# A fused attention and expert-lookup kernel: two of the four blocks of the input turned by transposing DMAs in the opening

## The chip, the cores and the metric

The kernel runs on one core of a Trainium2 chip. The metric is the device time of one execution in microseconds (us), lower is better. The core has five engines that work through instruction streams of their own and meet at semaphores: TensorE (PE; its weight loads are shown as PEld), VectorE (DVE), ScalarE (ACT), GpSimd (POOL) and SyncE (SP), from which nearly all DMAs are issued.

## The reference

```python
def _A_ref(x, wqkv, wo):                       # D = 448, 16 heads of 28
    qkv = (x @ wqkv).reshape(B, S, 3, H, Dh) ...
    p = softmax(einsum("bhqd,bhkd->bhqk", q, k) * Dh ** -0.5)
    return einsum("bhqk,bhkd->bhqd", p, v) ... @ wo
...
x = A_x                                        # 1 x 2048 x 448, float32
h = x + _A_ref(_layernorm(x), A_wqkv, A_wo)
h2 = h + _B_ref(_layernorm(h), ...)            # top-8 of 64 x 64 product keys per head,
                                               # gelu(x . u[e]) weighted, times v[e]
```

Only the opening is touched: layernorm of x, then keys, values and queries for the attention. Each fp32 factor of these products is carried as two fp16 parts (high and low), and a product is the sum of high*high, high*low and low*high.

## The kernel before

**Tiling.** The 2048 rows of x are four blocks of 512 rows, each of four tiles of 128 rows. `normed(b)` loads nothing; it takes a block that `load_x` has brought to `xb` (two buffers, so `load_x(b + 2)` stands at its end), makes mean and variance on VectorE (L395, L396), the reciprocal root on GpSimd (L110, L113) and the normalised tile `xn` on VectorE (L116). The products need x with features on the partitions, so each tile is turned: four TensorE transposes into PSUM (`turn`, L122, tile `tr`), the high parts by ScalarE from PSUM (L97, into `XH`), the low parts by VectorE from PSUM (`lows`, L136 and L137, into `XL` and into the free half of `XH`'s fourth slab).

**The order of the work.** `qkv()` normalises blocks 0 and 1. Then it runs over the four blocks: `keys(0, b)` (11 matmuls of 512 columns into `pq`; squares, a norm bound `kmax`, and the result split into `fh` and `fl` and stored) and, for blocks 0 and 1, `values_of(b)` (four times 11 matmuls of 448 columns, result `vst`, stored in `vd`). Blocks 2 and 3 are normalised inside that loop, ahead of `keys(0, 1)` and `keys(0, 2)`. The rest follows: `queries(0, b)`, then keys and queries of the other three groups of four heads, and the values of blocks 2 and 3 at the end. Keys of all four blocks must stand before the first query is finished, since `kmax` is taken over them. All of `qkv()` is laid out by a scheduler; it fixes an order per engine, GpSimd's alone is as written. Attention and all that comes after have an order written out by hand.

**Two helpers that stand ready.** `natural` (L127 to L130) splits a normalised tile where it lies, with its features along the free dimension: two casts for the high parts, two subtractions for the low ones, seven slabs of 128 columns in the order that `XH` and `XL` have. It is used later in the kernel (`project`), where a DMA of the transposing kind (L699) then turns those seven slabs, 128 rows x 896 columns of fp16 (229 KB), from SBUF to SBUF.

**Pools.** `wk` holds two buffers of each name (`bufs=2`) unless a tile asks for more: `xn` has two. `ps` holds two buffers of `tr` and four of `pq`.

## Time and profile before

| | us |
|---|---|
| median of 3 runs (lowest, highest) | 1591.58 (1589.65, 1596.7) |
| the profiled execution's own time | 1590.46 |
| its span, first to last instruction | 1588.7 |
| start of the first matmul of `keys(0, 1)` in that span | 37.9 |
| start of the first matmul of `keys(0, 2)` | 51.4 |
| start of the first matmul of `keys(0, 3)` | 55.2 |

The lines of the profile that carry the argument stand in the prediction. In them "L122 PE MATMUL tr<-ct,xn" is line, engine, operation, tile written <- tiles read (buffer numbers left out). Times at the start of a timeline row are us from the start of the span; "x4" groups instructions that follow each other; what stands in square brackets is the engine's idle time before the row, and what ended it. A row of a group ends with busy us and mean ns, or with the shortest, median and longest duration in ns. A DMA's row on SPq is the time that SyncE took to issue it; "to landing" counts from the start of that issue to the last completion.

### The profile page before, as it was taken

How to read it: one execution, taken by the hardware profiler on the slowest of the kernel's cores; microseconds unless marked ns; L12 is line 12 of the kernel's file. 1: busy time of each engine (PE TensorE's matmuls, PEld its weight loads, DVE VectorE, ACT ScalarE, POOL GpSimd, SP SyncE). 2: the span in 40 equal slices, each digit the busy share in tenths (PEclk: the TensorE clock that was granted, in tenths of full speed). 3: DMA queues.
4: the chain of work that ended last, by engine and by line, in shares of the span. 5: the costliest groups of instructions: out<-in, count | busy, mean ns of one | idle time of the engine just before them, and what ended most of it. 6: DMA issues, size and time to landing. Idle time of an engine off the chain costs nothing.

```text
span 1588.7 us, 33185 instructions
## 1 busy us (share of the span) xinstructions
PE 1532.8 (96%) x12540; PEld 669.4 (42%) x12540; DVE 1146.5 (72%) x3924; ACT 910.0 (57%) x1220; POOL 362.1 (23%) x488
## 2 busy tenths in 40 slices
PE   5999999999999999999998999999999999999999
PEld 3444222233333333333335654455445554555444
DVE  7763365444477867666599899789998999789623
ACT  3544888888888888888873433344423344334322
POOL 1242000534235743787662000000000000000000
PEclk9999999999999999999999999999999999999999
DMA  8424687556677756569733244453344534443444
GB/s 278 141 97 127 224 268 244 173 179 215 213 252 218 245 173 219 165 202 278 225 114 101 91 133 130 130 182 119 105 136 129 158 107 132 141 137 117 121 144 134
DMA packets 170018, 266.10 MB, mean 167 GB/s; under 512 B 25472, under 2 KB 102016, under 8 KB 169856
## 3 DMA queue, kind: packets, MB, share of 16 engines
q1 hardware_dynamic: 165632, 261.88, 52.9%
q10 hardware_dynamic: 4224, 2.10, 0.4%
q8 instruction: 98, 1.61, 0.4%
q14 instruction: 64, 0.52, 0.1%
HBM read 211.88 MB, written 49.28 MB: 164 GB/s over the span
## 4 chain that ended last, share of the span: by engine, by line
PE 74%; DVE 18%; DMA 2%; POOL 2%; issue 2%; ACT 1%; SPq 0%; DVEq 0%; POOLq 0%
PE M L93 14%; PE acc L1234 14%; PE A L592 13%; PE S L565 11%; PE A L93 9%; PE pq L93 6%; DVE p L994 4%; DVE fg L979 2%; DVE G L1015 2%; PE M L273 2%; PE A L1021 1%; DVE ring L1206 1%; DVE f L973 1%; DVE w L1209 1%; PE A L1011 1%
## 5 line engine op out<-in xcount | busy, mean ns | idle before, releaser
L569 ACT ACTIVATE P<-S,escale 128x1024 f32<-128x1024 f32 x512 | 535.7, 1118 | 82.1 <-PE S L565 75.9
L1234 PE MATMUL acc<-v,w 128*128 128x448 f16 x1536 | 308.3, 354 | 1.3 <-DVE w L1209 1.0
L592 PE MATMUL A<-P,V 128*32 128x512 f32 x2048 | 257.6, 601 | 1.3 <-DVE o L597 1.3
L565 PE MATMUL S<-qS,kS 32*128 32x512 f16 x3072 | 230.4, 378 | 2.9 <-ACT P L569 2.2
L1234 PEld LDWEIGHTS <-w 128*128 128x128 f16 x1536 | 148.4, 98 | 143.4 <-DVE w L1209 4.0
L93 PEld LDWEIGHTS <-u 128*128 128x128 f16 x1386 | 131.1, 98 | 146.4 <-issue 6.8
L93 PE MATMUL A<-Xb,u 128*128 128x512 f16 x759 | 178.6, 384 | 2.5 <-DVE G L1015 2.5
L1160 ACT ACTIVATE ring<-A,ugelu 128x512 f32<-128x512 f32 x71 | 48.7, 687 | 218.8 <-PE A L93 218.8
L994 DVE TENSOR_TENSOR p<-st,iota 128x2048 f16<-128x2048 f16 x128 | 156.7, 1225 | 14.9 <-PE M L1011 8.1
L93 PE MATMUL M<-w,Xb 128*128 128x512 f16 x704 | 163.1, 379 | 3.5 <-DVE oh L137 1.6
L1206 DVE SCALAR_TENSOR_TENSOR ring<-ring,wscale,G 128x512 f32<-128x512 f32 x128 | 92.1, 746 | 77.7 <-ACT ring L1160 77.6
L565 PEld LDWEIGHTS <-kS 32*128 32x128 f16 x3072 | 63.6, 92 | 198.3 <-issue 162.7
L93 PE MATMUL M<-Xb,u 128*128 128x512 f16 x627 | 146.4, 379 | 0.0
L93 PEld LDWEIGHTS <-Xb 128*128 128x128 f16 x704 | 64.0, 98 | 92.8 <-issue 20.5
L1208 ACT ACTIVATE w<-ring 128x512 f16<-128x512 f32 x128 | 75.8, 622 | 41.1 <-DVE ring L1206 28.9
L592 PEld LDWEIGHTS A<-P,V 128*32 128x32 f32 x2048 | 48.2, 108 | 120.5 <-issue 110.9
L816 DVE MAX8 ti<-fresh 128x8 f32<-128x64 f32 x384 | 57.3, 212 | 53.8 <-ACT fresh L797 53.6
L1051 POOL TENSOR_SCALAR raw<-raw,scale 128x512 f32<-128x512 f32 (+1 forms) x64 | 47.4, 741 | 188.7 <-PE M L158 145.8
L1209 DVE SCALAR_TENSOR_TENSOR w<-w,ring 128x512 f16<-128x512 f16 x128 | 84.9, 686 | 7.2 <-ACT w L1208 6.9
L1160 ACT ACTIVATE ring<-M,ugelu 128x512 f32<-128x512 f32 x57 | 39.2, 688 | 87.8 <-PE M L93 86.1
L979 DVE TENSOR_TENSOR fg<-f,st 128x2048 f16<-128x2048 f16 x64 | 78.8, 1231 | 0.1
L818 DVE FIND_INDEX8 ti<-ti,fresh 128x8 uint32<-128x64 f32 x384 | 76.9, 220 | 0.0
(197 smaller groups left out, 1897.3 us busy)
## 6 DMA issues: line engine op xcount, KB each, us to landing
v<-vs SPq DMA_DIRECT2D x128, 336.0 KB, 2.9
u<-us SPq DMA_DIRECT2D x126, 256.0 KB, 2.6
w<-wp SPq DMA_DIRECT2D x56, 512.0 KB, 4.9
kS<-ks SPq DMA_DIRECT2D x64, 256.0 KB, 4.9
V<-vd SPq DMA_DIRECT2D x64, 256.0 KB, 3.6
wr<-in_wq_dram SPq DMA_DIRECT2D x32, 448.0 KB, 4.2
vs<-hl SPq DMA_DIRECT2D x32, 336.0 KB, 5.2
seen<-in_uT_dram SPq DMA_DIRECT2D x32, 256.0 KB, 5.0
```

The costliest lines, as they stand in the source:

```text
L93: nc.tensor.matmul(ps, l, r, start=i == 0, stop=i == len(pairs) - 1)
L565: nc.tensor.matmul(S[j // 2][:, j % 2], kS[r, a, 128 * (k % 4):128 * (k % 4) + 128], qS[r, c], start=m == 0, stop=m == 2)
L569: nc.scalar.activation(Pt[:, 2 * i:2 * i + 2], S[i], AF.Exp, scale=escale[:, n % 4:n % 4 + 1])
L592: nc.tensor.matmul(O[n][32 * j:32 * j + 32], V[:, k % 4, j], Pt[:, j], start=k == 0, stop=k == NT - 1)
L818: nc.vector.max_index(i, t, src)
L979: nc.vector.tensor_tensor(fg.rearrange("p t k f u -> p t k (f u)"), f1.rearrange("p t f u -> p t (f u)").unsqueeze(2).to_broadcast([128, T ...
L994: newest[0] = nc.vector.tensor_tensor(p1, pairs(0, s, TG, 128), ids(TG, 128), op=OP.is_equal).ins
L1160: gelu[0] = nc.scalar.activation(act, p, AF.Gelu_apprx_tanh, scale=ugelu).ins
L1206: nc.vector.scalar_tensor_tensor(av, av, wscale, of_expert(b, f), op0=OP.mult, op1=OP.mult)
L1208: nc.scalar.activation(w[:, 0], a, AF.Copy, scale=1.0 / LS)
L1209: newest[0] = nc.vector.scalar_tensor_tensor(w[:, 1], w[:, 0], -LS, a, op0=OP.mult, op1=OP.add).ins
L1234: nc.tensor.matmul(acc[j][:, :D], l, r, start=f == 0 and k == 0, stop=f == 31 and k == 2)
```

## The change

Blocks 2 and 3 are no longer turned on TensorE. VectorE splits their tiles with `natural` into `hl`, a new tile of pool `wk` with two buffers, and a transposing DMA issued from SyncE turns each into `XT[b]`. `XH` and `XL` of a block become parts of one tile `XT`, so that one DMA can write both. Blocks 0 and 1 are turned as before. In the loop `normed(b + 2)` now stands between `keys(0, b)` and `values_of(b)` for blocks 0 and 1, and the keys of blocks 2 and 3 follow behind the values of block 1.

```diff
-        XH = [wp.tile([128, 4, 512], F16, name=f"XH{b}") for b in range(NB)]
-        XL = [wp.tile([128, 3, 512], F16, name=f"XL{b}") for b in range(NB)]
+        XT = [wp.tile([128, 7, 512], F16, name=f"XT{b}") for b in range(NB)]
+        XH = [t[:, :4] for t in XT]
+        XL = [t[:, 4:] for t in XT]
...
                 xn = wk.tile([128, D], F32, name="xn")
                 norm(xt[:, j], xn, mv[:, j, 0:1], rstd[:, j:j + 1], nc.vector)
+                if b > 1:
+                    hl = wk.tile([128, 7 * 128], F16, name="hl")
+                    natural(hl, xn)
+                    nc.sync.dma_start_transpose(XT[b][:, :, c], hl)
+                    continue
                 pt = ps.tile([128, 4, 128], F32, name="tr")
                 turn(pt, xn)
...
             normed(1)
-            for b in range(NB):
-                if b in (1, 2):
-                    normed(b + 1)
+            for b in range(2):
                 keys(0, b)
-                if b < 2:
-                    values_of(b)
+                normed(b + 2)
+                values_of(b)
+            for b in (2, 3):
+                keys(0, b)
```

What the scheduler makes of it is seen in the order of the instructions. Lines behind the edit have moved by one to six (L380 is L381, L395 and L396 are L396 and L397, L437 is L443). On VectorE before, in the middle of block 2, a tile is normalised and its low parts are taken from PSUM, waiting for ScalarE:

```order
L137 TENSOR_TENSOR XH_216<-tr,XH_216 64x128
L116 TENSOR_SCALAR xn<-xb,mv,rstd 128x448 [waits DVE_49]
L396 BN_AGGR mv<-st 128x2 [waits DVE_49]
L395 BN_STATS st<-xb 128x6 [waits DMAHW6_49]
L136 TENSOR_TENSOR XL_220<-tr,XH_216 128x3x128 [waits Activation_49]
```

On VectorE after, from the normalising of block 2's third tile on (the splits of the first two tiles stand just ahead of these rows):

```order
L116 TENSOR_SCALAR xn<-xb,mv,rstd 128x448
L116 TENSOR_SCALAR xn<-xb,mv,rstd 128x448 [waits DVE_49]
L397 BN_AGGR mv<-st 128x2 x2
L396 BN_STATS st<-xb 128x6 [waits DMAHW5_49]
L396 BN_STATS st<-xb 128x6 [waits DMAHW6_49]
L381 CAST fh<-f 128x512 [waits Activation_49]
L443 TENSOR_REDUCE kmax<-tr 128x1 [waits PE_49]
L127 CAST hl<-xn 128x384 [waits DMAHW7_49,DVE_49]
L128 CAST hl<-xn 128x64
L127 CAST hl<-xn 128x384 [waits DMAHW0_49,DVE_49]
L129 TENSOR_TENSOR hl<-xn,hl 128x384 [waits DVE_49]
L130 TENSOR_TENSOR hl<-xn,hl 128x64 [waits DVE_49]
```

The tiles are split in pairs, and each cast of 384 columns from the third tile on waits for a DMA semaphore: that of the transposing DMA that still reads this buffer of `hl`.

On SyncE before, behind the values of block 0:

```order
L419 DMA vd<-vst_225 128x4x128 [waits DMAHW6_49,Activation_49]
L260 DMA wr<-in_wq_dram 128x896 x2
L234 DMA V<-vd 128x512 [waits DMAHW4_49,DMAHW6_49,DMAHW2_49,DMAHW1_49]
L384 DMA ks_61<-fh 128x512 [waits DVE_49]
L385 DMA ks_61<-fl 128x512 [waits DMAHW3_49,Pool_49]
L419 DMA vd<-vst_222 128x4x128 [waits Activation_49]
```

And after, at the same place:

```order
L425 DMA vd<-vst_221 128x4x128 [waits DMAHW6_49,Activation_49]
L409 DMA_TRANSPOSE XT_216<-hl 128x7x128 [waits DVE_49] x2
L260 DMA wr<-in_wq_dram 128x896 [waits DMAHW1_49]
L385 DMA ks_61<-fh 128x512 [waits DMAHW2_49,DVE_49]
L386 DMA ks_61<-fl 128x512 [waits DMAHW3_49,Pool_49]
L425 DMA vd<-vst_218 128x4x128 [waits DMAHW4_49,Activation_49]
L409 DMA_TRANSPOSE XT_216<-hl 128x7x128 [waits DMAHW5_49,DVE_49]
L409 DMA_TRANSPOSE XT_216<-hl 128x7x128 [waits DMAHW6_49,DVE_49]
```

The second pair of block 2 stands behind the stores of `keys(0, 1)` and a store of `vst`. The four of block 3 (`XT_217`) follow further on, the last two with the store of `fh` of `keys(0, 2)` between them.

On TensorE before, in `keys(0, 2)`, the last transposes of block 3 stand between matmuls:

```order
L93 MATMUL pq<-XH_216,wqkl 128x512
L122 MATMUL tr<-ct,xn 128x128 [waits DVE_49,Activation_49]
L122 MATMUL tr<-ct,xn 128x128 x3
L93 LDWEIGHTS wqkh
L93 MATMUL pq<-XL_220,wqkh 128x512
```

After, at the end of `keys(0, 2)` and the start of `keys(0, 3)`:

```order
L93 LDWEIGHTS wqkh
L93 MATMUL pq<-XT_216,wqkh 128x512
L442 MATMUL tr<-sq,blk 128x512 [waits DVE_49,Activation_49]
L93 LDWEIGHTS wqkh [waits DMAHW4_49,DMAHW7_49,DMAHW3_49,DMAHW1_49]
L93 MATMUL pq<-XT_217,wqkh 128x512 [waits PE_49]
```

The transposes (L122) are gone, and the first weight load of `keys(0, 3)` waits for four DMA semaphores, those of the four transposing DMAs of block 3; that of `keys(0, 2)` waits for the four of block 2 in the same way. The order of all five engines is the same from the queries of group 0 on.

## The prediction

> **What bounds the kernel now.** I read the page first, then busy time by stretch of the opening, then the timeline of that stretch, the chain that ended last, and the groups of the tiles that the change touches. The page says that TensorE is the busy engine of the whole:

> ```profile
> span 1588.7 us, 33185 instructions
> PE 1532.8 (96%) x12540; PEld 669.4 (42%) x12540; DVE 1146.5 (72%) x3924; ACT 910.0 (57%) x1220; POOL 362.1 (23%) x488
> ```

> That is an average over all stages; the change lies between 36 and 62 us. Busy us per engine, with the count, in three stretches: from the normalising of block 2 to the end of the keys of group 0, the short passage to the queries, and the rest of keys and queries:

> ```profile
> 36.50:58.00 21.50, 20.72 (x112) 11.22 (x113) 16.58 (x41) 9.24 (x16) 2.63 (x4) 1.00 0.57 174
> 58.00:66.20 8.20, 6.51 (x31) 2.73 (x28) 4.83 (x14) 5.57 (x8) 2.06 (x2) 1.00 0.42 130
> 66.20:129.70 63.50, 63.50 (x279) 27.61 (x279) 44.07 (x96) 30.75 (x50) 27.76 (x24) 1.00 0.32 106
> ```

> The first number behind the length is TensorE: 20.72 of 21.50 us, then 6.51 of 8.20, then all of 63.50. VectorE (third number) has 4.9 us to spare in the first stretch, the DMA engines are 0.57 busy. The chain of waits says the same of the later part:

> ```profile
> 43.08 7.58 PE pq L93 x40
> ...
> 66.69 2.39 PE pq L93 x11
> ...
> 127.33 2.39 PE pq L93 x11
> ```

> From 66 us on it runs through one group of 11 matmuls after the other, with no step on another engine that a late start could be made up in. So whatever the keys of block 3 lose or win is lost or won at the end of the kernel too: the time at which `keys(0, 3)` ends decides. In the timeline:

> ```profile
> 35.09 0.73 PE L93 MATMUL pq<-wvh,XL 128*128 128x448 f16 x3
> 36.37 0.94 DVE L116 TENSOR_SCALAR xn<-xb,mv,rstd 128x448 f32<-128x448 f32 x2 [0.91 <-POOL rstd L113]
> 37.03 1.06 PE L122 MATMUL tr<-ct,xn 128*128 128x128 f32 x8 [1.20 <-DVE xn L116]
> ...
> 51.38 1.03 PE L93 MATMUL pq<-XH,wqkh 128*128 128x512 f16 x4
> ...
> 55.22 1.02 PE L93 MATMUL pq<-XH,wqkh 128*128 128x512 f16 x4
> ...
> 57.41 0.81 PE L93 MATMUL pq<-XL,wqkh 128*128 128x512 f16 x3
> ```

> The values of block 0 end at 35.82, TensorE waits 1.20 us for the normalised tile of block 2, `keys(0, 2)` starts at 51.38, `keys(0, 3)` at 55.22, and its last matmul ends at 58.22.

> **What is removed.** The transposes of blocks 2 and 3 and what hangs on them, in this stretch:

> ```profile
> L122 PE MATMUL tr<-ct,xn x32: 272/273/302, 37.0 to 54.3; 128*128 128x128 f32 x32
> L97 ACT ACTIVATE XH<-tr x8: 590/598/599, 37.7 to 54.6; 128x512 f16<-128x512 f32 x8
> L136 DVE TENSOR_TENSOR XL<-tr,XH x8: 551/558/559, 38.3 to 55.2; 128x384 f16<-128x384 f32 x8
> L137 DVE TENSOR_TENSOR XH<-tr,XH x8: 292/293/294, 38.9 to 55.8; 64x128 f16<-64x128 f32 x8
> L436 PE MATMUL tr<-sq,blk x2: 506/545/584, 42.6 to 55.9; 128*128 128x512 f32 x2
> ```

> TensorE loses 32 transposes. What that is worth I take from its new sequence. From 35.82 it can go straight to `keys(0, 1)` (11 matmuls, 2.39), one `blk` product (0.5) and the values of block 1 (44 matmuls at 7.58 / 40 = 0.19, 8.34): it is at `keys(0, 2)` by 47.05 instead of 51.38. If nothing made it wait, both keys would end at 47.05 + 2.39 + 0.5 + 2.39 = 52.33, that is 5.9 us before 58.22. This is all that the edit can win. ScalarE loses 8 x 0.60 us; that wins nothing, since it is busy for 9.24 of 21.50 us there.

> **What is added.** Per tile, four VectorE instructions in place of L136 and L137, and one transposing DMA. The same operations stand later in this kernel; the first four rows are the split, the fifth SyncE's time to issue the turn, the sixth from that issue's start to landing:

> ```profile
> L127 DVE CAST hl<-xn x12: 359/656/1200, 345.2 to 720.0; 128x384 f16<-128x384 f32 x12
> L128 DVE CAST hl<-xn x12: 176/408/2126, 345.8 to 720.5; 128x64 f16<-128x64 f32 x12
> L129 DVE TENSOR_TENSOR hl<-xn,hl x12: 545/552/951, 346.3 to 721.0; 128x384 f16<-128x384 f32 x12
> L130 DVE TENSOR_TENSOR hl<-xn,hl x12: 210/599/1189, 346.8 to 721.5; 128x64 f16<-128x64 f32 x12
> L699 SPq DMA_TRANSPOSE Xb<-hl x12: 1226/1237/1362, 350.8 to 725.4; - x12
> ...
> DMA to landing us min/median/max: 3.1/3.4/5.1
> ```

> I take the shortest durations (0.36, 0.18, 0.55, 0.21), because GpSimd is busy 2.63 of 21.5 us here and the long ones fall in a stage where it works beside VectorE (an inference). A tile costs 1.30 us instead of 0.85, over eight tiles 3.6 us more on VectorE, which the 4.9 spare us would cover. VectorE's load is not the trouble; its order is. There are two buffers of `hl`, so a pair of tiles can be split only after the pair before has landed, and four such rounds stand one behind the other. Between them VectorE does what the order puts there; the durations, and GpSimd's for the root (L113, L110) and for `fl`:

> ```profile
> L150 DVE TENSOR_REDUCE tops<-wqkr 128x1 f32<-128x512 f32 x4 | 2.6, 677 | 0.0
> L382 POOL TENSOR_TENSOR fl<-f,fh 128x512 f16<-128x512 f32 x2 | 2.3, 1162 | 18.9 <-DVE fh L380 18.9
> L437 DVE TENSOR_REDUCE kmax<-tr 128x1 f32<-128x512 f32 x2 | 1.4, 692 | 0.5 <-PE tr L436 0.4
> L395 DVE BATCH_NORM_STATS2 st<-xb 128x6 f32<-128x448 f32 x2 | 1.2, 594 | 0.0
> L113 POOL TENSOR_TENSOR rstd<-rstd,lnpow 128x4 f32<-128x4 f32 x1 | 1.0, 1012 | 0.1
> L380 DVE CAST fh<-f 128x512 f16<-128x512 f32 x2 | 0.8, 422 | 0.0
> L396 DVE BATCH_NORM_AGGREGATE mv<-st 128x2 f32<-128x6 f32 x4 | 0.6, 170 | 0.0
> L110 POOL TENSOR_SCALAR rstd<-mv 128x4 f32<-128x4 f32 x1 | 0.2, 195 | 0.1
> ```

> **The four rounds, with the median landing of 3.4.**
> - First pair. Two tiles normalised by 36.37 + 0.94 = 37.31. The order is cast, small cast, cast of the second tile, then the two subtractions: the first `hl` is ready 1.66 later at 38.97, the second after 0.94 more at 39.91. SyncE issues one turn in 1.24, so at 38.97 and 40.21; they land at 42.4 and 43.6.
> - Second pair. 39.91 + 0.94 (normalising) + 0.34 (two L396) + 1.19 (two L395) + 0.42 (`fh`) + 0.69 (`kmax`) = 43.49. Both buffers are just free. Ready at 45.15 and 46.09. Three stores stand ahead on SyncE (`fh`, `fl`, `vst`); they should be through before 45, since `fh` is made at 42.8 and GpSimd's `fl` 1.16 later. Issued at 45.15 and 46.39, landed at 48.55 and 49.8. TensorE has waited for `keys(0, 2)` since 47.05: **2.7 us lost**.
> - Third pair. 46.09 + 0.34, then GpSimd's 1.21 for block 3's root, 0.94 to normalise, two maxima of weights (2 x 0.68): 49.94, both landed. Ready at 51.60 and 52.54, issued at 51.60 and 52.84, landed at 55.0 and 56.2.
> - Fourth pair. 52.54 + 0.94 + 0.68 + three small ones (0.5, an estimate from L396's 0.17) = 54.66, and the buffer at 55.0. Ready at 56.30; the second tile's split has the cast of `fh` between its parts: 56.30 + 1.72 = 58.02. The last turn lands at 61.4. `keys(0, 2)` and its `blk` product are over by 52.7: **8.7 us lost**.

> `keys(0, 3)` ends at 61.42 + 2.39 = 63.8 instead of 58.2, **5.6 us later**; the same from TensorE's side is 2.7 + 8.7 lost less 5.9 won, 5.5. Successive VectorE instructions overlap a little (two normalisations take 0.94, one 0.51, so 0.08 each), and some of that lies on the path, for which I take off 0.6: **+5.0 us**. Behind it nothing changes: the squares, `kmax` and the scale of the next weights hang on the end of `keys(0, 3)` as before.

> Other edits. SyncE issues eight more DMAs, 9.9 us, beside the sum; the loads of `wr` behind them are for a later stage. The low share of GpSimd stays. One tile `XT` for two costs nothing: the readers wait for the same writers.

> **Bounds of the unknown, the landing.** The nearest rows are the twelve turns, 3.1 to 5.1, one at a time; here two follow each other, beside loads of `wr`. With 3.1 the same rounds give +5.0 (+4.4 with the overlap). With 5.1 every round waits for its landing: the turns land at 45.3, 52.8, 60.2 and 67.1 (the last of each pair), and the end comes 11.3 us later. Even at the shortest plain DMA of this size the rounds stand:

> ```profile
> h<-xt SPq DMA_DIRECT2D x12, 224.0 KB, 2.0
> xb<-in_x_dram SPq DMA_DIRECT2D x16, 224.0 KB, 4.2
> ```

> With a landing of 2.0, VectorE alone sets the rounds, and the sum is +3.9. I take 3.4, the median of the same instruction with the same size. [...]

> **The rivals.**
> - *The turns land late.* The place is the two waits for `hl` and the four DMAs that a key group waits for; behind the loads of `wr` each landing takes 4.3 or more instead of 3.4. From there the loss passes 8.0 us (at 4.2 it is 7.7), which is 0.5%, about what a measurement of this kernel can tell from no change. At 5.1 throughout, 1591.6 + 11.3 = 1602.9. For it: `wr` and the stores share the queue, and the DMA engines are 0.57 busy. Against it: half of the twelve turns landed within 3.4, and one late turn is not enough, it must be one in nearly every round.
> - *All is hidden.* TensorE never waits, and the 5.9 us are won: 1585.7. For it: VectorE has room, and a longer lead (the values of block 1, 8.3 us, stand between). Against it: the rounds above would have to be 9 us too long, and even a landing of 2.0 leaves +3.9.
> - *The loss is taken up behind.* Between 58 and 66.2 TensorE is idle for 8.20 - 6.51 = 1.7 us. If what it waits for there did not hang on `keys(0, 3)`, that much of the delay would vanish: 1594.9. Against it: the passage begins with the square of `keys(0, 3)` itself.
> - *The change does not do what it says.* Excluded: the order shows the DMAs in SyncE's stream and no L122 after block 1.

> **How the numbers follow.** The sum is made against the profiled execution (1590.46, span 1588.7); the median of the runs is 1.1 higher, and the difference is added to it: 1591.58 + 5.0 = **1596.6**. Chances: the forecast (landing of 3.1 to 4.3, 4 to 8 us later) 0.62; late 0.18; taken up behind 0.10; hidden 0.08; a gain beyond what the rows allow 0.02. The forecast, the third and the hidden case are all within 0.5%: same 0.80, slower 0.18, faster 0.02. The range leaves out the hidden case and the worst of the late one: 1591 to 1602.

> **What would show it.** Right: TensorE's first weight load of `keys(0, 2)` waits 2 to 3 us and that of `keys(0, 3)` 7 to 9 us for the DMA `XT<-hl`; VectorE's casts to `hl` begin close to 43.5, 50, 55; the turns land in 3.1 to 4.3 us; the values of block 1 end near 47; from the first query on all rows stand about 5 us later, to the end. Wrong: turns at 5 us or more, or a second turn that waits for the first; splits at their long durations (2.2 us a tile instead of 1.3, which would add about 0.9 in each of the last two rounds); or waits of TensorE that are gone by 66 us.

## The result, and the profile after

| | before | after |
|---|---|---|
| median of 8 runs each, us (lowest, highest) | 1593.06 (1589.65, 1596.7) | 1599.72 (1597.16, 1602.56) |
| the profiled execution's own time, us | 1590.46 | 1598.57 |
| its span, us | 1588.7 | 1596.8 |

The changed kernel takes 1.0036 times as long (95% interval 1.0025 to 1.0047): 0.36%, which is measured but lies within the 0.5% that was called no change. Of the kernel before there are now eight runs, and their median is 1.5 us above the one that the prediction started from.

The head of the page after:

```profile
span 1596.8 us, 33142 instructions
PE 1531.1 (96%) x12508; PEld 666.0 (42%) x12508; DVE 1149.7 (72%) x3940; ACT 906.1 (57%) x1212; POOL 362.0 (23%) x488
```

Every engine has about the same work as before, TensorE is busy for 1.7 us less, and the span is 8.1 us longer. So no engine got more to do; time was lost between pieces of it. Busy time by stretch after (behind the length: PE, PEld, DVE, ACT, POOL; then the granted TensorE clock, the DMA engines' share and GB/s):

```profile
36.50:58.00 21.50, 14.83 (x65) 6.47 (x63) 18.60 (x57) 4.89 (x8) 3.77 (x4) 0.83 0.99 231
58.00:62.50 4.50, 1.59 (x4) 0.57 (x5) 0.13 (x1) 0.00 (x0) 0.00 (x0) 0.50 0.83 189
62.50:72.00 9.50, 9.06 (x37) 3.70 (x35) 4.32 (x13) 4.58 (x7) 1.16 (x1) 0.91 0.17 55
72.00:135.00 63.00, 61.77 (x271) 26.86 (x272) 42.77 (x92) 31.13 (x51) 26.61 (x23) 1.00 0.33 108
```

TensorE is busy for 14.83 of the first 21.50 us (20.72 before). In the second stretch no compute engine has work to speak of until the last turn has landed; TensorE's 1.59 us stand at its end. And there is something that stood in none of the three rows of before: a clock of 0.83 and 0.50. From 72 us on the kernel runs as it did, only later. TensorE's timeline after shows where:

```profile
46.17 0.73 PE L93 MATMUL pq<-wvh,XT 128*128 128x448 f16 x3
49.25 1.02 PE L93 MATMUL pq<-XT,wqkh 128*128 128x512 f16 x4 [2.35 <-DMA XT<-hl]
...
53.58 0.80 PE L442 MATMUL tr<-sq,blk 128*128 128x512 f32 x1 [0.69 <-ACT sq L437]
60.91 1.89 PE L93 MATMUL pq<-XT,wqkh 128*128 128x512 f16 x4 [6.54 <-DMA XT<-hl]
62.59 1.82 PE L93 MATMUL pq<-XT,wqkl 128*128 128x512 f16 x4
64.25 1.67 PE L93 MATMUL pq<-XT,wqkh 128*128 128x512 f16 x7
...
73.04 0.49 PE L454 MATMUL tr<-sq,blk 128*128 128x512 f32 x1 [1.48 <-ACT sq L452]
```

The values of block 1 end at 46.90. Then `keys(0, 2)` waits 2.35 us and `keys(0, 3)` 6.54, both for the turning DMAs. Four matmuls take 1.02 us at 49.25 and 1.89 at 60.91. The chain of waits after (start, length, what) names the rounds that caused the two waits:

```profile
42.08 0.84 DVE hl L127
...
45.38 3.62 DMA XT<-hl
49.10 0.36 DVE hl L127
...
50.09 4.06 DMA XT<-hl
54.17 0.36 DVE hl L127
...
57.55 3.31 DMA XT<-hl
60.91 5.01 PE pq L93 x15
```

A landing releases a cast into `hl`, its split releases the next turn, and the next landing again a cast: this chain holds the stretch from 45.4 to 60.9, and at its end stands `keys(0, 3)`. The same instruction (ScalarE's first square of a query) starts at 61.0 before and 68.0 after, 7.1 us later; the first softmax row of the attention at 156.2 and 163.4, 7.2 later. That row, before and after:

```profile
156.21 2.12 ACT L569 ACTIVATE P<-S,escale 128x1024 f32<-128x1024 f32 x2 [0.91 <-PE S L565]
163.37 6.38 ACT L575 ACTIVATE P<-S,escale 128x1024 f32<-128x1024 f32 x6 [0.91 <-PE S L571]
```

### The profile page after: what moved, and what is told of

Same layout as the page of the kernel before. It is cut to its first block, busy times and chain, and to the rows that moved or that the text cites. A ratio compares the mean times of both kernels' runs of the same rounds, so it can differ in the third digit from the quotient of the medians.

```text
span 1596.8 us, 33142 instructions
## 1 busy us (share of the span) xinstructions
PE 1531.1 (96%) x12508; PEld 666.0 (42%) x12508; DVE 1149.7 (72%) x3940; ACT 906.1 (57%) x1212; POOL 362.0 (23%) x488
## 4 chain that ended last, share of the span: by engine, by line
PE 64%; DVE 22%; POOL 6%; DMA 4%; issue 2%; ACT 1%; SPq 0%; DVEq 0%; POOLq 0%; ACTq 0%
PE acc L1240 13%; PE M L93 12%; PE A L598 10%; PE S L571 9%; PE A L93 8%; PE pq L93 5%; DVE p L1000 4%; DVE G L1021 2%; DVE fg L985 2%; PE M L273 2%; DVE ring L1212 2%; POOL sel L879 2%; DVE pos L824 1%; DVE w L1215 1%; POOL sel L883 1%
## 5 line engine op out<-in xcount | busy, mean ns | idle before, releaser
L93 PEld LDWEIGHTS <-u 128*128 128x128 f16 x1386 | 130.8, 98 | 145.7 <-issue 5.3
L93 PE MATMUL A<-Xb,u 128*128 128x512 f16 x759 | 175.7, 380 | 2.4 <-DVE G L1021 2.4
L93 PE MATMUL M<-w,Xb 128*128 128x512 f16 x704 | 163.1, 379 | 6.2 <-DMA w<-wp 4.2
L93 PE MATMUL M<-Xb,u 128*128 128x512 f16 x627 | 147.9, 382 | 0.0
L93 PEld LDWEIGHTS <-Xb 128*128 128x128 f16 x704 | 64.1, 98 | 95.5 <-issue 23.3
```

The lines of the kernel that those rows point to most:

```text
L93: nc.tensor.matmul(ps, l, r, start=i == 0, stop=i == len(pairs) - 1)
```

## The experiments

Delays are those of the same instruction against the profile of before. "Turns" is when the last turning DMA landed, the waits are TensorE's at `keys(0, 2)` and at `keys(0, 3)`, and "half clock" is the time at 0.5 between 36 and 80 us. Ratios are to the kernel before, on the same chip in each group of four.

| kernel | turns | waits | half clock | first softmax row | median us | ratio (95%) |
|---|---|---|---|---|---|---|
| the changed kernel | 60.9 | 2.35, 6.54 | 13.7 | +7.2 | 1599.72 | 1.0036 (1.0025, 1.0047) |
| e1: eight buffers of `hl` | 57.4 | 0.52, 6.21 | 10.2 | +4.5 | 1595.68 | 1.0019 (1.0010, 1.0028) |
| e2: work in the waits | 60.0 | none, 0.82 | 0 | +4.7 | 1597.49 | 1.0029 (1.0017, 1.0041) |
| e3: the new order alone | – | none there | 0 | +1.5 | 1594.22 | 1.0004 (0.9989, 1.0018) |
| e4: block 2 alone turned by DMA | 49.2 | none there | 3.4 | +0.7 | 1592.84 | 0.9996 (0.9986, 1.0005) |
| e5: one buffer of `hl` | 74.2 | 9.98, 10.38 | 27.3 | +20.2 | 1614.18 | 1.0116 (1.0097, 1.0135) |
| e6: values of block 2 in the hole | 61.9 | 2.42, 1.12 | 0 | -1.7 | 1591.46 | 0.9984 (0.9973, 0.9995) |
| e7: e6 with eight buffers | 60.1 | 0.39, 1.31 | 0 | -3.4 | 1587.72 | 0.9969 (0.9956, 0.9983) |
| e8: the kernel before, so filled | – | none there | 0 | +0.5 | 1593.14 | 1.0000 (0.9988, 1.0013) |

**e1: eight buffers of `hl`.** The suspected cause, taken away: no cast waits for a landing any more.

```diff
-                    hl = wk.tile([128, 7 * 128], F16, name="hl")
+                    hl = wk.tile([128, 7 * 128], F16, name="hl", bufs=8)
```

> The changed kernel with eight buffers of hl instead of two; nothing else is edited. Theory 1 (rounds): the late keys of block 3 come from four rounds of split, turn and landing that two buffers force one behind the other. With eight, the scheduler puts both pairs of a block's splits side by side: the turns of block 2 should land by 47, so TensorE does not wait for keys(0, 2), and the last turn of block 3 should land near 56.4 instead of 60.9. keys(0, 3) then ends near 60.5 (still at half clock) instead of 65.0: 4.5 us faster than the changed kernel, about 2 us slower than before. Rival (SyncE): the loss is the 9.9 us that SyncE takes to issue eight turns, in which case more buffers win nothing and the time stays about 6 us above before.

The wait at `keys(0, 2)` fell from 2.35 to 0.52 and the last turn landed 3.5 us earlier, so the two buffers did hold the rounds. They did it in two ways that this run does not part: by casts that waited for a landing, and by the order that the scheduler made for two buffers. With eight it splits the second pair of block 2 ahead of `fh`, `kmax` and the last statistics of block 3, and SyncE issues it at 42.1 instead of 44.0. The gain is smaller than expected: the attention starts 2.6 us earlier than in the changed kernel, where 4.5 had been expected of the whole time; the last landing was hoped for at 56.4 and came at 57.4. `keys(0, 3)` ran at half clock, as expected. Rows of e1, of VectorE's, SyncE's and TensorE's timeline and of the busy time:

```profile
46.43 0.94 DVE L116 TENSOR_SCALAR xn<-xb,mv,rstd 128x448 f32<-128x448 f32 x2 [0.84 <-POOL rstd L113]
51.79 1.16 SPq L425 DMA_DIRECT2D vd<-vst  x2
53.05 2.67 SPq L409 DMA_TRANSPOSE XT<-hl  x2
57.51 1.87 PE L93 MATMUL pq<-XT,wqkh 128*128 128x512 f16 x4 [6.21 <-DMA XT<-hl]
52.50:62.70 10.20, 5.19 (x13) 1.91 (x14) 2.00 (x6) 0.24 (x1) 1.15 (x1) 0.50 0.93 227
```

With the buffers free, block 3 waits for GpSimd's reciprocal root until 46.43, and its last pair of turns stands on SyncE behind two stores of `vst`. So the buffers are the first cause, and a wait of 6.21 us is left. The late start of block 3 looks like the next one; no run moved it, so that is not shown.

**e2: work in the waits.** The turns stay as they are; TensorE repeats the products of `keys(0, 0)`, whose results nobody reads, once ahead of `keys(0, 2)` and three times ahead of `keys(0, 3)`.

```diff
             for b in (2, 3):
+                for n in range(1 if b == 2 else 3):
+                    proj(wqks[0][0], 0)
                 keys(0, b)
```

> The changed kernel with 11 matmuls of block 0 once more ahead of keys(0, 2) and 33 ahead of keys(0, 3), whose results nobody reads: TensorE has something to do while it waits. Theory 1 (wait, then half clock): the last turn lands as late as in the changed kernel, near 60.9, but the granted clock stays at 1.0, so keys(0, 3) takes 2.4 us instead of 4.1; 1.7 us faster than the changed kernel, some 4 to 5 us slower than before. Rival (the longer matmuls of keys(0, 3) have another cause, such as the DMA traffic at that time): keys(0, 3) still takes 4 us and the time is that of the changed kernel or more.

TensorE and the busy time of e2:

```profile
60.06 1.04 PE L93 MATMUL pq<-XT,wqkh 128*128 128x512 f16 x4 [0.82 <-DMA XT<-hl]
60.94 1.03 PE L93 MATMUL pq<-XT,wqkl 128*128 128x512 f16 x4
61.80 1.67 PE L93 MATMUL pq<-XT,wqkh 128*128 128x512 f16 x7
50.50:64.20 13.70, 12.88 (x59) 5.66 (x58) 5.22 (x19) 2.35 (x4) 1.15 (x1) 1.00 0.91 214
```

The same stretch of the changed kernel, and the one behind it:

```profile
50.50:64.20 13.70, 6.47 (x15) 2.06 (x14) 5.92 (x18) 1.18 (x2) 1.40 (x1) 0.50 0.92 209
64.20:72.00 7.80, 7.36 (x33) 3.11 (x31) 4.32 (x13) 4.58 (x7) 1.16 (x1) 1.00 0.10 34
```

The DMA share is the same (0.91 and 0.92), TensorE's idleness isn't (0.82 and 7.23 of 13.70 us; ahead of it, from 40.0 to 50.5, none and 2.35), and the clock is 1.00 instead of 0.50. So the clock fell for the idleness, not for the traffic. The first eight matmuls of `keys(0, 3)` take 61.80 - 60.06 = 1.74 us, in the changed kernel 64.25 - 60.91 = 3.34: 1.6 us were the clock's. The other 0.9 of the 2.5 us gained in the opening come from the last turn, which landed at 60.0. Against the medians (1599.72 and 1597.49, of different chips) the 2.2 us fit, but the intervals overlap; the shift within the traces carries this reading.

**e3: the new order alone**, and **e4: block 2 alone turned by DMA.** In e3 no block is turned by DMA (the tile `XT` and the new order stay), in e4 only block 2.

```diff
-                if b > 1:
+                if b > 9:        # e3
+                if b == 2:       # e4
```

> The changed kernel's order of the loop and its tile XT, but blocks 2 and 3 turned on TensorE as before: no split where the tiles lie, no turning DMA. Theory 1: the order alone costs nothing; keys(0, 3) ends between 56.5 and 58.5 and the time is within 2 us of before, that is 5 to 7 us faster than the changed kernel. Rival (order): the keys of blocks 2 and 3 behind the values, and the normalising ahead of them, are the loss; then this stays 4 us or more above before.

> The changed kernel with block 2 turned by DMAs and block 3 turned on TensorE. Theory 1 (rounds): two rounds are over when TensorE gets there, the other two are what is late. The turns of block 2 land near 49 as in the changed kernel, block 3's 16 transposes take 1.8 us of TensorE in the time in which it would wait for them, keys(0, 3) ends near 54.5 at full clock: 3 to 4 us faster than before, about 9 faster than the changed kernel. Rival (any turning DMA in the opening delays TensorE by what SyncE and the queue take): half of the loss stays, 3 us slower than before.

Order and tile alone cost 1.5 us in the opening and nothing that the runs can tell: the rival that the new order is the loss falls. In e4 I had looked for a gain of 3.5 us; it is 0.7 late. One row of TensorE each, e3 and then e4:

```profile
47.37 1.06 PE L122 MATMUL tr<-ct,xn 128*128 128x128 f32 x8 [1.67 <-DVE xn L116]
47.13 1.12 PE L122 MATMUL tr<-ct,xn 128*128 128x128 f32 x8 [2.95 <-DVE xn L116]
```

The transposes of block 3 stand among the values of block 1, and TensorE comes to them before block 3 is normalised (its root again). In e4, which has less to do on TensorE, it comes earlier and waits 2.95 instead of 1.67 us. Behind that wait the clock falls for 3.4 us (TensorE is slow from 48.1 to 51.5):

```profile
48.80 2.07 PE L93 MATMUL pq<-wvh,XT 128*128 128x448 f16 x5
```

Five matmuls take 2.07 us here; seven of the same form take 1.49 at full clock. Most of what the DMA saves for block 2 is lost to the longer wait and to the half clock behind it.

**e5: one buffer of `hl`.** The suspected cause, doubled.

```diff
-                    hl = wk.tile([128, 7 * 128], F16, name="hl")
+                    hl = wk.tile([128, 7 * 128], F16, name="hl", bufs=1)
```

> The changed kernel with one buffer of hl instead of two. Theory of the rounds: now each tile's split waits until the turn before it has landed, so eight rounds of 1.3 us (split) and 3.0 us (issue to landing, the fastest turns of the changed kernel) stand one behind the other: first turn issued at 38.5, last landing near 38.5 + 3.1 + 7 x 4.3 = 71.7 instead of 60.9, the first query's square about 10 us later than in the changed kernel, and 1600 + 11 = 1610 us. TensorE waits about 15 us in the two places together, twice what it waits in the changed kernel. Rival (what delays the turns is the DMA queue or SyncE, not the buffers): the turns are as many and as large as before, and with fewer of them at a time each lands sooner; the end moves by less than 3 us.

```profile
57.58 1.86 PE L93 MATMUL pq<-XT,wqkh 128*128 128x512 f16 x4 [9.98 <-DMA XT<-hl]
74.29 1.87 PE L93 MATMUL pq<-XT,wqkh 128*128 128x512 f16 x4 [10.38 <-DMA XT<-hl]
49.70:77.00 27.30, 8.35 (x19) 2.80 (x20) 8.50 (x25) 1.18 (x2) 1.15 (x1) 0.50 0.51 115
```

These are two rows of TensorE and one of busy time. The rival (queue or SyncE) falls: the turns are the same eight, their median landing is shorter (2.9 us instead of 3.5), the DMA share is lower, and the attention starts 13 us later than in the changed kernel. The size was missed upward, 1614 instead of 1610: a round took 4.6 us on average instead of 4.3 (first issue 39.0, last 71.3, seven rounds). The last turn landed at 74.2, 13.3 us later than in the changed kernel, and that is the whole delay. The 27.3 us at half clock add nothing to it: the first eight matmuls of `keys(0, 3)` take 3.0 us here and 3.34 in the changed kernel, and what else runs at half clock there, `keys(0, 2)`, is followed by a wait for the turns anyway.

**e6: the values of block 2 in the hole.** No work is added: 44 matmuls move from the end of the opening to between the two keys.

```diff
-            for b in (2, 3):
-                keys(0, b)
+            keys(0, 2)
+            values_of(2)
+            keys(0, 3)
...
-            for b in range(2, NB):
-                values_of(b)
+            values_of(3)
```

> The changed kernel with the values of block 2 (44 matmuls, 8.3 us) moved from the end of the opening to the place between keys(0, 2) and keys(0, 3). Theory (the loss is TensorE idle in the hole, and the clock that falls with the idleness): values of block 2 run from 51.7 to about 60.2, the wait at keys(0, 3) shrinks from 6.5 us to under 1, and the granted clock comes back before 60; keys(0, 3) ends near 63.5. Behind it the same work is 8.3 us shorter, so the attention starts about 8 us sooner than in the changed kernel: 1592, ratio to the kernel before 0.999 (0.998 to 1.001). If the clock stays at half through the values (it fell at 50.5 in the changed kernel), they take up to 16.7 us and the gain is nothing: 1600. Rival (the opening's end is set by something else than TensorE's work, the checks and loads ahead of the attention): what is moved away from there is not missed, and the time stays at 1598.

```profile
49.57 1.02 PE L93 MATMUL pq<-XT,wqkh 128*128 128x512 f16 x4 [2.42 <-DMA XT<-hl]
61.99 1.04 PE L93 MATMUL pq<-XT,wqkh 128*128 128x512 f16 x4 [1.12 <-DMA XT<-hl]
```

The wait at `keys(0, 3)` shrinks from 6.54 to 1.12 (under 1 was expected), its matmuls run at full clock (1.04 us instead of 1.89), and the attention starts 8.9 us earlier than in the changed kernel. The ratio is 0.9984: the loss is gone, and a little of the gain that the transposes promised is there. That the clock did not fall at all (1.00 from 36.5 to 72 us), though TensorE waited 2.42 us at `keys(0, 2)`, may be luck of this execution (an inference, see the last section); how often it falls there in others was not measured.

**e7: the same with eight buffers.** Both parts together, against the remaining wait at `keys(0, 2)`.

> The same filling, with eight buffers of hl. With eight buffers the last turn landed at 57.4; the values of block 2 run from 50.5 to about 58.9, so keys(0, 3) starts without a wait and TensorE works through from the values of block 0 on but for about 0.5 us at keys(0, 2). Theory: the 5.9 us of transposes and waits that the change took off TensorE are then won, less 0.5 and perhaps 1.5 us of half clock: 1593.4 - 5 = 1588.4, ratio 0.997 (0.996 to 0.998), faster than both kernels. Rival (the loss lies in the DMA traffic of the opening, which slows stores and loads for later stages): the traffic is the same, and the time stays above 1593.

```profile
47.64 1.02 PE L93 MATMUL pq<-XT,wqkh 128*128 128x512 f16 x4 [0.39 <-DMA XT<-hl]
...
60.25 1.02 PE L93 MATMUL pq<-XT,wqkh 128*128 128x512 f16 x4 [1.31 <-DMA XT<-hl]
```

1587.72 us, 0.9969 of the kernel before (0.9956 to 0.9983), 1588.4 expected: this version beats both kernels, the one before by 0.3%. Its turns land later than in e1 (60.1, the slowest took 5.6 us) and `keys(0, 3)` is not free of a wait, as had been expected, but the values of block 2 cover all of that but 1.31 us.

**e8: the control.** The kernel before, its transposes on TensorE, with `values_of(2)` at the same place.

> A control: the kernel before, with its transposes on TensorE, and the values of block 2 moved to the same place. Theory: TensorE had no wait at keys(0, 3) there that they could fill, so moving them wins nothing: ratio 1.000 (0.9985 to 1.001). Rival (the values of block 2 cost more at the end of the opening than in it, so that moving them is a gain of its own): 0.998 or less, and the gain of the filled kernels would not be the hole's.

```profile
63.56 0.73 PE L93 MATMUL pq<-wvh,XL 128*128 128x448 f16 x3
64.13 1.03 PE L93 MATMUL pq<-XH,wqkh 128*128 128x512 f16 x4
```

There was no wait to fill (the keys follow the values without one), and nothing is won: 1.0000. So e6 and e7 gain by the hole, not by the move.

## Why the prediction was right

It said 1596.6 (1591 to 1602) and "within 0.5%"; it is 1599.72, 0.36% slower by the ratio. The rounds came close to what was worked out; one thing that lengthened the end of the path was not seen. Of the 3.1 us between the two numbers, 1.5 are the higher median of the kernel before, and the rest is about what the half clock cost. That the class held in spite of it is in part luck: 0.5% left 3 us of room above the sum.

- **The bound.** "The time at which `keys(0, 3)` ends decides": right. The delay at the first query (+7.1) stands unchanged at the attention (+7.2). "The loss is taken up behind" fell: the wait ahead of the queries' norm is 1.48 us at 73.04, and before it was 1.69:

```profile
66.19 0.49 PE L448 MATMUL tr<-sq,blk 128*128 128x512 f32 x1 [1.69 <-ACT sq L446]
```

- **Splits and landings.** The rows after, as a group:

```profile
L127 DVE CAST hl<-xn x8: 347/354/932, 37.2 to 55.2; 128x384 f16<-128x384 f32 x8
L128 DVE CAST hl<-xn x8: 180/186/190, 37.4 to 55.4; 128x64 f16<-128x64 f32 x8
L129 DVE TENSOR_TENSOR hl<-xn,hl x8: 544/552/559, 37.8 to 55.9; 128x384 f16<-128x384 f32 x8
L130 DVE TENSOR_TENSOR hl<-xn,hl x8: 210/218/1173, 38.3 to 56.4; 128x64 f16<-128x64 f32 x8
L409 SPq DMA_TRANSPOSE XT<-hl x8: 1221/1256/1544, 38.5 to 57.6; - x8
...
DMA to landing us min/median/max: 2.9/3.5/4.1
```

The short durations were the right choice, and the landing's median is 3.5 for the 3.4 taken. The inference behind the choice fits its exceptions: the two long ones lie beside GpSimd's two subtractions for `fl`. No run tests it.

```profile
42.08 0.93 DVE L127 CAST hl<-xn 128x384 f16<-128x384 f32 x1
56.35 1.17 DVE L130 TENSOR_TENSOR hl<-xn,hl 128x64 f16<-128x64 f32 x1
41.63 1.16 POOL L383 TENSOR_TENSOR fl<-f,fh 128x512 f16<-128x512 f32 x1 [5.37 <-DVE fh L381]
56.04 1.40 POOL L383 TENSOR_TENSOR fl<-f,fh 128x512 f16<-128x512 f32 x1 [9.82 <-DVE fh L381]
```

- **The four rounds.** Issued at 38.97, 45.15 (this one's second at 46.39), 51.60 and 58.02 (the last) by the sum; 38.5, 44.0 (45.4), 50.1 and 57.6 in the trace. The last landing was put at 61.4, less 0.6 of overlap, and came at 60.9. VectorE's own order set the first two rounds and all but 0.35 us of the third, as worked out. The fourth waited 1.70 us for its landing where the sum had 0.3 (54.66 to 55.0), since VectorE came to it at 52.5. The first three pairs were issued 0.5 to 1.5 us earlier than in the sum, and from the third pair's issue to the last one it took 7.5 us instead of 6.4; that the last landing comes out within 0.1 us is in part luck.
- **TensorE's losses.** 2.7 us at `keys(0, 2)`: 2.35. For `keys(0, 3)` 8.7: the last wait is 6.54, and 0.69 lies ahead of the `blk` product before it; the rest was eaten by the matmuls between, those of `keys(0, 2)`, which ran slower.
- **The term that failed** is the length of `keys(0, 3)`, put at "2.39" as before; the prediction says nothing of the clock. At half clock its first eight matmuls alone took 1.6 us longer (against e2). With +5.0 this makes +6.6 of the +7.1 seen at the first query.
- **Rivals.** Late turns did not come (the slowest of the eight took 4.1 us, where 4.3 or more was named). All hidden: refuted here, and reached in part by e7 with other work in the hole. In other runs turns took longer, up to 5.6 us in e7. The rows of plain transfers of this size (224 KB) in the profile of before have medians from 2.0 to 4.9.

The profile after is 8.1 us longer than the one before, the medians 6.7. Most of the difference of 1.4 is one more stretch of 3.4 us at half clock, at 166.6 us, at the start of the attention: there the delay goes from 7.2 to 8.5 and stays. The profile of before has no such stretch there. Of the runs, e6 and e7 are granted 0.96 from 120 to 165 us, which is about one such stretch. What stays open is how often it is there: e8, in which nothing waits for a turning DMA, is granted 0.92 in the same window (about two of them), so it does not hang on the change.

## What to carry to other kernels

Work taken off the bounding engine and handed to DMAs was worth here only what its latency left (5.9 us of TensorE's time against waits of 2.35 and 6.54): count the buffers between producer and DMA as rounds of split and landing (from the start of the issue) before counting what is saved. If a hole remains, look for work of the same engine that is ready and stands later (here the values of block 2, 8.3 us); moving it into the hole turned 1.0036 into 0.9984, and with more buffers into 0.9969. The holes in TensorE's stream also cost clock here (0.50 from 50.5 to 64.2 us): add what the matmuls behind a hole take at half clock (the first eight of `keys(0, 3)` 3.34 us instead of 1.74).

## What the hardware showed that was not expected

This is not a threshold for the whole kernel. In the profiles of before and after, from some 20 us on, where the record of the clock begins, every interval at full clock with 2.0 us or more of idleness was followed by half clock (before: 2.08 us from 1336.0; after: 2.13 from 47.1, 2.21 from 1084.8 and 2.21 from 1344.2; both: the last 3.4 us of the span, in which TensorE has no work), but between 1.0 and 2.0 both are found: after has 1.95 us (from 787.8) without a fall and 1.78 (from 163.2) with one, and before falls behind an interval with 1.28 (from 919.6), in a stage of 64 small matmuls (128x32). What besides idleness counts there stays open.
